# Two steps of a long convolution, interleaved in batches of four units instead of two

## The chip, the cores and the metric

The kernel runs on one core of one Trainium2 chip. The metric is the device time of one launch in microseconds (us). TensorE (PE) multiplies, VectorE (DVE), ScalarE (ACT) and GpSimd (POOL) work element by element, and SyncE (SP) issues the transfers between memory and the chip's SBUF. PE writes its results to PSUM, which has eight banks of 2 KB per partition; ACT and DVE read them from there.

## The reference

Two stages follow one another. The change touches the first one only, a long convolution by Fourier transform:

```python
h_mlp = np.maximum(pos_emb @ w1, 0.0) @ w2        # the filter
u = x * v                                         # (4, 11456, 128)
Uf = np.fft.rfft(u, n=2 * S, axis=1)
Hf = np.fft.rfft(h_mlp * window, n=2 * S, axis=0)
y = np.fft.irfft(Uf * Hf[None], n=2 * S, axis=1)[:, :S, :]
attn_out = x * y
```

The second stage is a soft mixture of eight experts over the 45,824 rows of `attn_out`. All data are float32.

## The kernel before

The transform has length 111 x 197 and is done as matrix products with tables, in four steps for each of G = 8 groups of 16 channels (64 rows of batch and channel). A group's 64 rows are worked on as NU = 16 *units* of four.

- **Step 1** (`first`, matmuls on L138, copies in `first_out` on L150) transforms a unit of `u` along one axis. The operands are at most 64 x 64, so four matmuls run side by side in the four quarters of PE's array. A unit is 16 matmuls into two PSUM banks, and ACT copies each bank to the SBUF tile T.
- **Step 2** (`p2`, L279) transforms along the other axis, four columns of T at a time; DVE multiplies with the filter's spectrum Hs (L282), and POOL writes the sums back into T (L287, L288).
- **Step 3** (`p3`, matmuls L296, copies L302) is the inverse along the second axis: 8 matmuls a unit on nearly the full array (111 x 99) into two banks, each copied by ACT to the tile E.
- **Step 4** (`p4`, L331) is the inverse along the first; ACT and DVE finish it (`p4_copy` L340, `p4_gate` L345 to L356), and the result is written out.

The trace has two PE records for every matmul of the program, so a unit of step 3 is 16 records and a unit of step 1 is 32.

For g = 1 to 7, the loop first runs **step 3 of group g-1 and step 1 of group g interleaved** (below: the 3/1 stage), because a unit of step 1 writes the part of T that two units of step 3 have read. Then steps 4 of group g-1 and 2 of group g alternate (the 4/2 stage). Group 8 has only steps 3 and 4 left. Nearly every instruction is marked to keep the order in which the program writes it, so the order of each engine is the order of the code; engines wait for one another by semaphores.

In the 3/1 stage before, units go in pairs: step 3 for units 2b and 2b+1, then step 1 for the same two, for b = 0 to 7. (For b = 0, step 1's matmuls come ahead.) Behind each unit u of step 3, DVE prepares the input of step 1's unit u+2 (`p1_sd`: L229, twice L231, twice L235); behind each unit u of step 1, SP asks for x of unit u+6 (`p1_x`, L223), or of the next group's first two units. The ring `ld` of six buffers ties x of unit u+6 to the end of step 1's unit u. From b = 4 on, SP also asks for nine pieces of the group's spectrum (L391), and at the stage's end for v of the next group's first two units (L213); then DVE prepares these two units as well, ahead of its first multiplication of step 2.

PSUM is divided for good: pool `psa` has four tiles of one bank, which step 1 and step 2 use, and pool `pso` has two tiles of two banks, which step 3 and step 4 use. A tile is given out again when its last reader has finished, so step 1's unit u waits for the copies of unit u-2, and so does step 3's.

Of the kernel before, what the change touches and what calls it, by code (L numbers as in the profile page):

```python
# [11 lines left out]
F32 = mybir.dt.float32  # L12
F32R = mybir.dt.float32r
AF = mybir.ActivationFunctionType
# [7 lines left out]
J = 99  # L22
# [3 lines left out]
R = 56  # L26
RP = 64
FO = 64
G = 8
# [32 lines left out]
def conv_part(ctx, tc, cp, moe, xf, vf, xi, xe, pos, w1, w2, win, t1x, t1h, wt, t3, t4, hs, scr):  # L62
# [64 lines left out]
        eng.tensor_tensor(out=hid[:, 0, rs], in0=hb[:, :, 0], in1=hb[:, :, 1], op=ALU.add)  # L127
        nc.vector.tensor_tensor(out=hid[:, 1, rs], in0=hb[:, :, 0], in1=hb[:, :, 1], op=ALU.subtract)

    def first(g, u, sd):  # L130

        ps = [psa.tile([128, 2, 2, J], F32, tag="psa", name=f"p1_{g}_{u}_{h}") for h in range(2)]
        for i in range(2):
            for s in range(2):
                for h in range(2):
                    js = slice(RP * h, RP * h + JH)
                    for d in range(2):
                        steady(g, nc.tensor.matmul(  # L138
                            ps[h][RP * d : RP * d + RP, i, s, :], lhsT=sd[js, i, s, d, :],
                            rhs=tab1x[js, J * (s + d) : J * (s + d + 1)],  # L140
                            start=True, stop=True, tile_position=(RP * h, RP * d)))
        return ps

    def first_out(g, u, ps):

        for h in range(2):
            dst = T[:, :, 2 * (u % 2) + h, u // 2]
            src = ps[h].rearrange("p c s k -> p s k c")
            if g or h == 0:
                steady(g, nc.scalar.activation(dst, src, AF.Copy))  # L150
            else:
                inorder(nc.vector.tensor_copy(out=dst, in_=src))
# [51 lines left out]
    def p1_v(g, u):  # L204
        k = u % HV if g == 0 else u - PRE
        if 0 <= k < HV:
            vt = Hs.rearrange("p k x -> p (k x)")[:, 8 * R * k : 8 * R * k + 8 * R]
        elif HV <= k < NU - 3:
            vt = m_half(g, k - HV)[:, : 8 * R]
        else:  # L210
            vt = ld.tile([128, 8 * R], F32, tag="lv", name=f"v_{g}_{u}", bufs=2)
        vt = vt.rearrange("p (c q r) -> p c q r", c=2, q=4)
        inorder(nc.sync.dma_start(out=vt, in_=vf[g, u]))  # L213
        vts[u] = vt

    def p1_x(g, u):
        if g == 0 and u < NU // 2:
            xt = moe.E[:, J * N1 + 8 * RP * u :][:, : 8 * RP].rearrange("p (c q r) -> p c q r", c=2, q=4)
        elif g == 0 and u >= NU - 2:
            xt = m_half(g, u).rearrange("p (c q r) -> p c q r", c=2, q=4)  # L220
        else:
            xt = ld.tile([128, 2, 4, RP], F32, tag="ld", name=f"x_{g}_{u}")
        inorder(nc.sync.dma_start(out=xt, in_=xf[g, u]))  # L223
        xts[u] = xt

    def p1_sd(g, u, eng):
        xt, vt = xts.pop(u), vts.pop(u)
        xr = xt[:, :, :, :R]
        inorder(eng.tensor_tensor(out=xr, in0=xr, in1=vt, op=ALU.mult))  # L229
        for m, op in ((0, ALU.add), (2, ALU.subtract)):  # L230
            inorder(eng.tensor_tensor(out=vt[:, :, m : m + 2], in0=xr[:, :, 0:2], in1=xr[:, :, 2:4], op=op))  # L231
        sd = xt.rearrange("p c (s d) r -> p c s d r", s=2)
        vq = vt.rearrange("p c (s q) r -> p c s q r", s=2)
        for d, op in ((0, ALU.add), (1, ALU.subtract)):
            inorder(eng.tensor_tensor(out=sd[:, :, :, d, :R], in0=vq[:, :, :, 0], in1=vq[:, :, :, 1],  # L235
                                      op=op))
        return sd
# [30 lines left out]
    for k in range(0, J, 4):  # L268
        filter_second(k)

    def p1(g, u, sd):
        first_out(g, u, first(g, u, sd))

    def p2(g, k0):
        n = min(KB, J - k0)
# [11 lines left out]
        inorder(nc.gpsimd.tensor_tensor(out=Ty[:, 0], in0=m[:, :n, 0, 0], in1=m[:, :n, 1, 1], op=ALU.subtract))  # L287
        inorder(nc.gpsimd.tensor_tensor(out=Ty[:, 1], in0=m[:, :n, 1, 0], in1=m[:, :n, 0, 1], op=ALU.add))  # L288

    def p3(g, u):  # L290
        ps = pso[0].tile([J, 2, 512], F32, tag="psb", name=f"p3_{g}_{u}")
        for k in range(2):
            pk = ps[:, k, : 8 * R].rearrange("p (i q r) -> p i q r", i=2, q=4)
            for i in range(2):
                for s in range(2):
                    inorder(nc.tensor.matmul(pk[:, i, 2 * s : 2 * s + 2, :].rearrange("p q r -> p (q r)"),  # L296
                                             lhsT=T[0:N1, s, 2 * k + i, u // 2, :, u % 2],
                                             rhs=tab3[:, 2 * R * s : 2 * R * (s + 1)],
                                             start=True, stop=True))
        for k in range(2):  # L300
            c = 4 * u + 2 * k
            inorder(nc.scalar.activation(  # L302
                E[:J, :, :, c : c + 2].rearrange("p r q c -> p q r c"),
                ps[:, k, : 8 * R].rearrange("p (i q r) -> p q r i", i=2, q=4), AF.Copy))

    AINV = pow(N1, -1, N2)

# [71 lines left out]
    for g in range(G + 1):  # L379

        if g == 0:
            for u in range(NU):
                p1(g, u, sds.pop(u))
        elif g < G:
            if not pso:
                first_ps.close()
                pso.append(ctx.enter_context(tc.tile_pool(name="pso", bufs=2, space=bass.MemoryType.PSUM)))
            for b in range(NU // 2):
                if b >= 4:
                    for k in range(11 * (2 * b - 8), min(J, 11 * (2 * b - 5 if b == 7 else 2 * b - 6)), 11):  # L390
                        inorder(nc.sync.dma_start(out=Hs[:, k : k + 11], in_=hs[g, :, k : k + 11]))  # L391
                us = (2 * b, 2 * b + 1)
                ps = {u: first(g, u, sds[u]) for u in us if b == 0}
                for u in us:
                    p3(g - 1, u)
                    if u + 2 < NU:
                        sds[u + 2] = p1_sd(g, u + 2, nc.vector)
                for u in us:
                    if b:
                        ps[u] = first(g, u, sds[u])  # L400
                    first_out(g, u, ps[u])
                    w = u + 6
                    if w < NU:
                        p1_x(g, w)
                    elif w < NU + PRE and g + 1 < G:
                        p1_x(g + 1, w - NU)
                if b == 0:
                    for w in range(PRE + HV, NU):
                        p1_v(g, w)
                if b == NU // 2 - 1 and g + 1 < G:  # L410
                    for w in range(PRE):
                        p1_v(g + 1, w)
# [641 lines left out]
```

## Time and profile before

| | us |
|---|---|
| runs: median (lowest, highest) of 3 | 947.03 (944.58, 947.36) |
| profiled execution, its own time | 946.41 |
| span of the profiled execution | 944.6 |
| one 3/1 stage and one 4/2 stage (224.00 to 262.43 and 262.43 to 307.19) | 38.43 and 44.76 |

The profile shows one execution on one core. A row of the timeline gives the start in us, the time from the first start to the last end of a run of like instructions, the engine, the line, the operation, what it writes and reads, the shape, the number of records, and in brackets the idle time ahead of it with what ended it. PEld is PE's loading of weights, which overlaps PE. The granted clock of TensorE is 0.983 of full speed on the mean over the span and 1.00 in both stages named in the table. The names are shortened there: p is any PSUM tile.

### The profile page before, as it was taken

Reading aid. Unit: us, or ns where it says so; the run is one execution under the profiler, and the core shown is the slowest. Engines: PE = TensorE matmul, PEld = TensorE weight load, DVE = VectorE, ACT = ScalarE, POOL = GpSimd, SP = SyncE. Lnnn points to the kernel's source line nnn. Section 1 sums busy time; section 2 is a strip of 40 time slices with the busy share of each in tenths; the row PEclk is TensorE's granted clock in tenths of the full one; section 3 lists DMA queues with packets and bytes.
Section 4 is the critical chain, followed back from the end, with each engine's and each line's share of the span. In section 5 each row is a group of like instructions: output and inputs, shape, how many; then the busy total and the mean of one; then the engine's idle time right before and its main releaser. Section 6 shows DMA issues by size and latency. Waiting matters only on the chain. (4 is left out here: it accounts for less than half of the span.)

```text
span 944.6 us, 32994 instructions
## 1 busy us (share of the span) xinstructions
PE 900.0 (95%) x14040; PEld 813.9 (86%) x14040; DVE 734.7 (78%) x1282; ACT 445.3 (47%) x964; POOL 381.8 (40%) x582
## 2 busy tenths in 40 slices
PE   6999999999999999999999999999999989999991
PEld 5998889999999999999999999999998987776540
DVE  7935769699789879978988998898697068876781
ACT  0655447514721751472166137216612548887561
POOL 5001760183058018405800840581085006876810
PEclk9999999999999999999999999999999999999995
DMA  8923985456745855673585568358435888775598
GB/s 267 394 71 104 325 284 173 156 169 206 240 123 160 266 156 156 194 258 111 161 274 168 152 181 257 106 173 268 142 99 164 290 300 296 259 264 158 208 417 372
DMA packets 104239, 201.18 MB, mean 213 GB/s; under 512 B 14167, under 2 KB 65577, under 8 KB 100252
## 3 DMA queue, kind: packets, MB, share of 16 engines
q1 hardware_dynamic: 103806, 198.89, 63.9%
q8 instruction: 111, 1.82, 0.8%
q14 instruction: 36, 0.29, 0.1%
q10 hardware_dynamic: 254, 0.11, 0.0%
q0 software_dynamic: 32, 0.07, 0.0%
HBM read 139.12 MB, written 59.90 MB: 211 GB/s over the span
## 5 line engine op out<-in xcount | busy, mean ns | idle before, releaser
L287 POOL TENSOR_TENSOR T<-m 111x256 f32<-111x256 f32 (+1 forms) x200 | 148.0, 740 | 424.1 <-DVE m L282 424.1
L282 DVE TENSOR_TENSOR m<-p,T 111x1024 f32<-111x1024 f32 (+1 forms) x175 | 200.1, 1207 | 22.1 <-PE p L279 21.2
L296 PE MATMUL p<-tab,T 111*99 111x112 f32 x2048 | 211.4, 262 | 2.3 <-DVE E L356 1.6
L296 PEld LDWEIGHTS p<-tab,T 111*99 111x99 f32 x2048 | 201.3, 171 | 9.7 <-issue 2.9
L279 PE MATMUL p<-T,W 128*111 128x128 f32 x1584 | 194.7, 278 | 0.0
L279 PEld LDWEIGHTS p<-T,W 128*111 128x111 f32 x1584 | 183.0, 173 | 7.3
L340 ACT ACTIVATE vc<-p 128x416 f32<-128x416 f32 x112 | 51.8, 515 | 283.9 <-DVE p L345 192.5
L331 PE MATMUL p<-tab,E 99*64 99x104 f32 x3584 | 171.9, 253 | 2.2 <-ACT E L302 1.1
L302 ACT ACTIVATE E<-p 99x448 f32<-99x448 f32 x256 | 130.5, 575 | 83.5 <-PE p L296 83.5
L331 PEld LDWEIGHTS p<-tab,E 99*64 99x64 f32 x3584 | 161.3, 136 | 9.8 <-issue 1.7
L288 POOL TENSOR_TENSOR T<-m 111x256 f32<-111x256 f32 (+1 forms) x200 | 146.6, 733 | 0.0
L150 ACT ACTIVATE T<-p 128x396 f32<-128x396 f32 x240 | 102.3, 530 | 6.7 <-PE p L138 6.6
L138 PE MATMUL p<-tab1x,x 53*64 53x99 f32 x3776 | 96.5, 248 | 3.3 <-issue 1.7
L138 PEld LDWEIGHTS p<-tab1x,x 53*64 53x64 f32 x3776 | 84.7, 133 | 10.4 <-issue 2.0
L345 DVE TENSOR_TENSOR p<-p,vc 128x832 f32<-128x832 f32 x56 | 57.4, 1025 | 14.2 <-ACT vc L340 14.2
L560 ACT ACTIVATE xreg<-pt 128x512 f32<-128x512 f32 x90 | 48.0, 602 | 5.9 <-PE pt L559 3.9
L229 DVE TENSOR_TENSOR x<-x,T 128x448 f32<-128x448 f32 x55 | 34.1, 620 | 19.7 <-DMA x<-in_xf_dram 18.8
L353 DVE TENSOR_TENSOR E<-p,E 128x824 f32<-128x824 f32 x46 | 46.8, 1017 | 1.6
L559 PE MATMUL pt<-ident,xreg 128*128 128x128 f32 x358 | 47.5, 278 | 0.0
L661 POOL TENSOR_TENSOR E<-lt,mx 128x512 f32<-128x512 f32 (+1 forms) x23 | 23.5, 1024 | 58.9 <-ACT et L642 58.9
L559 PEld LDWEIGHTS pt<-ident,xreg 128*128 128x128 f32 x358 | 40.1, 146 | 4.9 <-issue 2.4
L282 DVE TENSOR_TENSOR m<-p,E 111x1024 f32<-111x1024 f32 (+1 forms) x25 | 29.0, 1208 | 19.4 <-ACT E L186 15.3
(108 smaller groups left out, 966.6 us busy)
## 6 DMA issues: line engine op xcount, KB each, us to landing
x<-in_xf_dram SPq DMA_DIRECT2D x118, 256.0 KB, 4.1
out_dram<-xreg SPq DMA_DIRECT2D x21, 1024.0 KB, 9.6
E<-in_xi_dram SPq DMA_DIRECT2D x46, 412.0 KB, 3.6
scr<-E SPq DMA_DIRECT2D x84, 206.0 KB, 3.3
T<-in_vf_dram SPq DMA_DIRECT2D x65, 224.0 KB, 5.3
hs<-E SPq DMA_DIRECT2D x12, 1024.0 KB, 5.1
T<-hs SPq DMA_DIRECT2D x63, 176.0 KB, 3.7
mv<-in_vf_dram SPq DMA_DIRECT2D x42, 224.0 KB, 5.1
```

Of the source, the lines that this page charges most:

```text
L138: steady(g, nc.tensor.matmul(ps[h][RP * d : RP * d + RP, i, s, :], lhsT=sd[js, i, s, d, :], rhs=tab1x[js, J * (s + d) : J * (s + d + 1)], ...
L150: steady(g, nc.scalar.activation(dst, src, AF.Copy))
L279: steady(g, nc.tensor.matmul(ps[:, i].rearrange("p b c -> p (b c)"), lhsT=W[:, k0 + i, :], rhs=Tf[:, :, k0 + i, :], start=True, stop=True))
L282: inorder(nc.vector.tensor_mul(m[:, :n].rearrange("p k s e c i -> p k s (e c i)").rearrange("p k s (b c) -> p k s b c", c=CG), ps[:, :n].u ...
L287: inorder(nc.gpsimd.tensor_tensor(out=Ty[:, 0], in0=m[:, :n, 0, 0], in1=m[:, :n, 1, 1], op=ALU.subtract))
L288: inorder(nc.gpsimd.tensor_tensor(out=Ty[:, 1], in0=m[:, :n, 1, 0], in1=m[:, :n, 0, 1], op=ALU.add))
L296: inorder(nc.tensor.matmul(pk[:, i, 2 * s : 2 * s + 2, :].rearrange("p q r -> p (q r)"), lhsT=T[0:N1, s, 2 * k + i, u // 2, :, u % 2], rhs ...
L302: inorder(nc.scalar.activation(E[:J, :, :, c : c + 2].rearrange("p r q c -> p q r c"), ps[:, k, : 8 * R].rearrange("p (i q r) -> p q r i", ...
L331: inorder(nc.tensor.matmul(pv[RP * h : RP * h + RP, 2 * k + i, w, :], lhsT=E[:J, r, 2 - 2 * w + s, :], rhs=tab4[:, s, o : o + NJ], start=( ...
L340: inorder(nc.scalar.activation(vc[:, w], pv[:, :, 0, :], AF.Copy, scale=2.0 * w - 1.0))
L345: inorder(nc.vector.tensor_tensor(out=pw, in0=pw[:, 1:2].to_broadcast([128, 2, 4, NJ]), in1=vc, op=ALU.add))
L559: inorder(nc.tensor.transpose(pt[:, j, :], self.xt[i][:, k + j, :], self.ident))
```

## The change

In the 3/1 stage, units now go in batches of four: step 3 for units 4b to 4b+3, then step 1 for the same four, for b = 1 to 3. The first four units keep their order of two and two. To have eight banks for a batch, both steps now take tiles of both pools: the first two units of a batch take one two-bank tile of `pso` each, the other two take two one-bank tiles of `psa` each. Steps 2 and 4, and step 3 of the last group, take what they took. The pieces of the spectrum are asked for four at the start of b = 2 and five at the start of b = 3.

```diff
+    def banks(g, u, name, large):
+        if large:
+            t = pso[0].tile([128, 2, 512], F32, tag="psb", name=f"{name}_{g}_{u}")
+            return [t[:, h] for h in range(2)]
+        return [psa.tile([128, 512], F32, tag="psa", name=f"{name}_{g}_{u}_{h}") for h in range(2)]
+
-    def first(g, u, sd):
+    def first(g, u, sd, large=False):
-        ps = [psa.tile([128, 2, 2, J], F32, tag="psa", name=f"p1_{g}_{u}_{h}") for h in range(2)]
+        ps = [t[:, : 4 * J].rearrange("p (c s k) -> p c s k", c=2, s=2) for t in banks(g, u, "p1", large)]
...
-    def p3(g, u):
-        ps = pso[0].tile([J, 2, 512], F32, tag="psb", name=f"p3_{g}_{u}")
+    def p3(g, u, large=True):
+        ps = [t[:J, : 8 * R] for t in banks(g, u, "p3", large)]
...
-            for b in range(NU // 2):
-                if b >= 4:
-                    for k in range(11 * (2 * b - 8), min(J, 11 * (2 * b - 5 if b == 7 else 2 * b - 6)), 11):
-                        inorder(nc.sync.dma_start(out=Hs[:, k : k + 11], in_=hs[g, :, k : k + 11]))
-                us = (2 * b, 2 * b + 1)
-                ps = {u: first(g, u, sds[u]) for u in us if b == 0}
-                for u in us:
-                    p3(g - 1, u)
-                    if u + 2 < NU:
-                        sds[u + 2] = p1_sd(g, u + 2, nc.vector)
-                for u in us:
-                    if b:
-                        ps[u] = first(g, u, sds[u])
-                    first_out(g, u, ps[u])
...
+            def third(us, larges):
+                for u, large in zip(us, larges):
+                    p3(g - 1, u, large)
                     if u + 2 < NU:
                         sds[u + 2] = p1_sd(g, u + 2, nc.vector)
...
+            third(range(2, 4), (True, True))
+            for u in range(2, 4):
+                p1(g, u, sds[u])
+                behind(u)
+            for b in range(1, NU // 4):
+                if b > 1:
+                    spectrum(4 * b - 8, 5 * b - 6)
+                us = range(4 * b, 4 * b + 4)
+                third(us, (True, True, False, False))
+                for u in us:
+                    p1(g, u, sds[u], u % 4 < 2)
+                    behind(u)
```

`behind(u)` holds the loads of x that stood in the old loop, `spectrum` the loads of Hs.

How PE's own order changes is shown where the old order left units 4 and 5 (group 2). Here `p1_2_5` is step 1 of group 2, unit 5 (the last digit after it, if any, is the bank), and `p3_1_6` is step 3 of group 1, unit 6. Before:

```order
L138 MATMUL p1_2_5_0_2984<-tab1x_74,x_2_5_2405 64x99 x2
L138 MATMUL p1_2_5_1_2985<-tab1x_74,x_2_5_2405 64x99 x2
L296 MATMUL p3_1_6_3006<-tab3_75,T_78 99x112 x8
L296 MATMUL p3_1_7_3022<-tab3_75,T_78 99x112 x8
L138 MATMUL p1_2_6_0_3038<-tab1x_74,x_2_6_2837 64x99 x2
L138 MATMUL p1_2_6_1_3039<-tab1x_74,x_2_6_2837 64x99 x2
```

Now, from the batch's first unit to its first two units of step 1:

```order
L302 MATMUL p3_1_4_2930<-tab3_75,T_78 99x112 x8
L302 MATMUL p3_1_5_2946<-tab3_75,T_78 99x112 x8
L302 MATMUL p3_1_6_0_2962<-tab3_75,T_78 99x112 x4
L302 MATMUL p3_1_6_1_2963<-tab3_75,T_78 99x112 x4
L302 MATMUL p3_1_7_0_2979<-tab3_75,T_78 99x112 x4
L302 MATMUL p3_1_7_1_2980<-tab3_75,T_78 99x112 x4
L144 MATMUL p1_2_4_2996<-tab1x_74,x_2_4_2403 64x99 x16
L144 MATMUL p1_2_5_3017<-tab1x_74,x_2_5_2405 64x99 x16
```

Units 6 and 7 of step 3 moved ahead of units 4 and 5 of step 1 and write one-bank tiles. The number of matmuls is what it was.

ACT's copies of units 4 to 7 follow the same pattern. Before:

```order
L302 ACTIVATE E_79<-p3_1_4_2930 99x4x56x2 x2
L302 ACTIVATE E_79<-p3_1_5_2946 99x4x56x2 x2
L150 ACTIVATE T_78<-p1_2_4_0_2962 128x2x198
L150 ACTIVATE T_78<-p1_2_4_1_2963 128x2x198
L150 ACTIVATE T_78<-p1_2_5_0_2984 128x2x198
L150 ACTIVATE T_78<-p1_2_5_1_2985 128x2x198
L302 ACTIVATE E_79<-p3_1_6_3006 99x4x56x2 x2
L302 ACTIVATE E_79<-p3_1_7_3022 99x4x56x2 x2
L150 ACTIVATE T_78<-p1_2_6_0_3038 128x2x198
L150 ACTIVATE T_78<-p1_2_6_1_3039 128x2x198
```

Now:

```order
L308 ACTIVATE E_79<-p3_1_4_2930 99x4x56x2 x2
L308 ACTIVATE E_79<-p3_1_5_2946 99x4x56x2 x2
L308 ACTIVATE E_79<-p3_1_6_0_2962 99x4x56x2
L308 ACTIVATE E_79<-p3_1_6_1_2963 99x4x56x2
L308 ACTIVATE E_79<-p3_1_7_0_2979 99x4x56x2
L308 ACTIVATE E_79<-p3_1_7_1_2980 99x4x56x2
L156 ACTIVATE T_78<-p1_2_4_2996 128x2x198 x2
L156 ACTIVATE T_78<-p1_2_5_3017 128x2x198 x2
L156 ACTIVATE T_78<-p1_2_6_0_3038 128x2x198
L156 ACTIVATE T_78<-p1_2_6_1_3039 128x2x198
```

Eight copies to E now stand ahead of eight to T, where four and four alternated.

On SP, the second half of the stage before, where `x_2_14` is x of group 2, unit 14, and `x_3_0` that of the next group:

```order
L223 DMA x_2_13_3080<-in_xf_dram 128x512
L391 DMA T_78<-hs_57 128x352 x2
L223 DMA x_2_14_3136<-in_xf_dram 128x512
L223 DMA x_2_15_3158<-in_xf_dram 128x512
L391 DMA T_78<-hs_57 128x352 x2
L223 DMA x_3_0_3214<-in_xf_dram 128x512
L223 DMA x_3_1_3236<-in_xf_dram 128x512
L391 DMA T_78<-hs_57 128x352 x5
L213 DMA v_3_0_3377<-in_vf_dram 128x448
```

Now:

```order
L229 DMA x_2_13_3080<-in_xf_dram 128x512
L409 DMA T_78<-hs_57 128x352 x4
L229 DMA x_2_14_3171<-in_xf_dram 128x512
L229 DMA x_2_15_3192<-in_xf_dram 128x512
L229 DMA x_3_0_3214<-in_xf_dram 128x512
L229 DMA x_3_1_3236<-in_xf_dram 128x512
L409 DMA T_78<-hs_57 128x352 x5
L219 DMA v_3_0_3377<-in_vf_dram 128x448
```

Two pieces of the spectrum moved ahead of x of units 14 and 15; the five pieces behind x of the next group stand where they stood.

More of the change, by code (lines that the diff above doesn't have):

```diff
@@ L269, in conv_part, with p1 @@
         filter_second(k)
-    def p1(g, u, sd):
-        first_out(g, u, first(g, u, sd))
+    def p1(g, u, sd, large=False):
+        first_out(g, u, first(g, u, sd, large))
     def p2(g, k0):
@@ L288, in p2 @@
         inorder(nc.gpsimd.tensor_tensor(out=Ty[:, 1], in0=m[:, :n, 1, 0], in1=m[:, :n, 0, 1], op=ALU.add))
-    def p3(g, u):
-        ps = pso[0].tile([J, 2, 512], F32, tag="psb", name=f"p3_{g}_{u}")
+    def p3(g, u, large=True):
+        ps = [t[:J, : 8 * R] for t in banks(g, u, "p3", large)]
         for k in range(2):
-            pk = ps[:, k, : 8 * R].rearrange("p (i q r) -> p i q r", i=2, q=4)
+            pk = ps[k].rearrange("p (i q r) -> p i q r", i=2, q=4)
             for i in range(2):
@@ L303, in p3 @@
                 E[:J, :, :, c : c + 2].rearrange("p r q c -> p q r c"),
-                ps[:, k, : 8 * R].rearrange("p (i q r) -> p q r i", i=2, q=4), AF.Copy))
+                ps[k].rearrange("p (i q r) -> p q r i", i=2, q=4), AF.Copy))
     AINV = pow(N1, -1, N2)
@@ L396, in conv_part @@
                     if u + 2 < NU:
                         sds[u + 2] = p1_sd(g, u + 2, nc.vector)
-                for u in us:
-                    if b:
-                        ps[u] = first(g, u, sds[u])
-                    first_out(g, u, ps[u])
[L402 to L409, printed above, removed]
@@ L410, in conv_part, with behind, spectrum @@
-                if b == NU // 2 - 1 and g + 1 < G:
-                    for w in range(PRE):
-                        p1_v(g + 1, w)
+            def behind(u):
+                w = u + 6
+                if w < NU:
+                    p1_x(g, w)
+                elif w < NU + PRE and g + 1 < G:
+                    p1_x(g + 1, w - NU)
+            def spectrum(i0, i1):
+                for k in range(11 * i0, 11 * i1, 11):
+                    inorder(nc.sync.dma_start(out=Hs[:, k : k + 11], in_=hs[g, :, k : k + 11]))
@@ new lines, in conv_part @@
+            ps = [first(g, u, sds[u]) for u in range(2)]
+            third(range(2), (True, True))
+            for u in range(2):
+                first_out(g, u, ps[u])
+                behind(u)
+            for w in range(PRE + HV, NU):
+                p1_v(g, w)
+            third(range(2, 4), (True, True))
[7 more added lines that the diff above has]
+                third(us, (True, True, False, False))
+                for u in us:
+                    p1(g, u, sds[u], u % 4 < 2)
+                    behind(u)
@@ L413, in conv_part @@
+            if g + 1 < G:
+                for w in range(PRE):
+                    p1_v(g + 1, w)
         else:
```

## The prediction

> **What bounds the kernel now.** I read the engines' shares on the page first, then the busy time by stage, then PE's timeline through one 3/1 stage, then the engines that could hold PE up there.
>
> ```profile
> PE 900.0 (95%) x14040; PEld 813.9 (86%) x14040; DVE 734.7 (78%) x1282; ACT 445.3 (47%) x964; POOL 381.8 (40%) x582
> ```
>
> ```profile
> 224.00:262.43 38.43, 38.31 (x770) 36.38 (x768) 31.81 (x82) 28.32 (x64) 0.32 (x1) 1.00 0.77 249
> 262.43:307.19 44.76, 44.76 (x650) 42.99 (x646) 41.78 (x44) 6.70 (x15) 34.18 (x50) 1.00 0.47 137
> ```
>
> The second fence gives, per stretch, its length and then the busy time of PE, PEld, DVE, ACT and POOL. PE is busy all through both stages (38.31 of 38.43, 44.76 of 44.76), so whatever shortens PE's own work there shortens the kernel, until another engine takes over. DVE is the nearest: 31.81 and 41.78.
>
> A busy PE may still lose time between its instructions, which is where this change acts:
>
> ```profile
> 224.00 1.61 PE L138 MATMUL p<-tab1x,x 53*64 53x99 f32 x64
> 225.53 6.72 PE L296 MATMUL p<-tab,T 111*99 111x112 f32 x64
> 232.18 1.61 PE L138 MATMUL p<-tab1x,x 53*64 53x99 f32 x64
> 233.72 3.32 PE L296 MATMUL p<-tab,T 111*99 111x112 f32 x32
> 236.97 1.61 PE L138 MATMUL p<-tab1x,x 53*64 53x99 f32 x64
> 238.51 3.31 PE L296 MATMUL p<-tab,T 111*99 111x112 f32 x32
> ...
> 260.89 1.61 PE L138 MATMUL p<-tab1x,x 53*64 53x99 f32 x64
> 262.43 3.08 PE L331 MATMUL p<-tab,E 99*64 99x104 f32 x64
> ```
>
> From one step-1 run to the next a pair takes (260.89 - 232.18) / 6 = 4.785 us: 3.25 from the start of step 3 to that of step 1, and 1.54 back. How much of it is matmul? These rows are pieces from inside a run, and the long run of step 3 in the last group, which no step 1 interrupts:
>
> ```profile
> 234.29 2.46 PE L296 MATMUL p<-tab,T 111*99 111x112 f32 x24
> 237.11 1.30 PE L138 MATMUL p<-tab1x,x 53*64 53x99 f32 x52
> 726.94 23.22 PE L296 MATMUL p<-tab,T 111*99 111x112 f32 x240 [0.91 <-DVE E L356]
> L296 PE MATMUL p<-tab,T x2048: 259/259/507, 141.5 to 749.9; 111*99 111x112 f32 x187
> L138 PE MATMUL p<-tab1x,x x3776: 242/244/370, 76.8 to 678.6; 53*64 53x99 f32 x199
> ```
>
> A record of step 3 takes 0.259 us from start to end, so 24 of them start (2.46 - 0.26) / 23 = 0.0957 us apart; over 240 it is 0.0961. Step 1's records start in fours: 52 are 13 fours, and the step from four to four is between (1.30 - 0.24) x 4 / 51 = 0.083 and (1.30 - 0.24) / 12 = 0.088; I take 0.086. A pair is then 32 x 0.0957 + 16 x 0.086 = 3.06 + 1.38 = 4.44 us of matmul. **The other 0.345 us (0.31 to 0.39 by the two bounds) is what changing from step 3 to step 1 and back costs.** It is no wait for data: it is the same in every pair, and the copies that the next run needs are long done, as follows.
>
> **What the change removes.** The matmuls stay the same 14,040 records. Before, each stage goes back and forth seven times after the first run (b = 1 to 7); now four times (units 2-3, then three batches). Three round trips fewer, in seven stages: 21 x 0.345 = **7.2 us** (6.5 to 8.2). A batch takes 64 x 0.0957 + 32 x 0.086 + 0.345 = 9.22 us in place of 9.57.
>
> **What it moves on ACT and PSUM.** Now a batch's step-1 units want the banks of its step-3 units, and the next batch's step 3 those of step 1.
>
> ```profile
> 233.42 1.74 ACT L150 ACTIVATE T<-p 128x396 f32<-128x396 f32 x4
> 235.55 1.02 ACT L302 ACTIVATE E<-p 99x448 f32<-99x448 f32 x2 [0.38 <-PE p L296]
> 237.08 1.04 ACT L302 ACTIVATE E<-p 99x448 f32<-99x448 f32 x2 [0.51 <-PE p L296]
> 237.99 1.67 ACT L150 ACTIVATE T<-p 128x396 f32<-128x396 f32 x4
> ```
>
> A unit's two copies to E take 1.04 us and start 0.11 after PE's run of step 3 (237.08 against 236.97); its two copies to T take half of 1.67, 0.84. Counted from a batch's start, step 1 begins at 3.25 + 32 x 0.0957 = 6.31. The fourth unit's copies to E end at 6.42 + 1.04 = 7.46, and its banks are wanted again by step 1's fourth unit at 6.31 + 0.73 + 2 x 0.69 = 8.42 (8 fours, 0.69 us a unit, and 0.04 more for the first): 0.96 to spare. Copies to T end at 8.30, 9.14, 9.98 and 10.82; the next batch's four step-3 units want those tiles at 9.22, 10.76, 12.29 and 13.82: 0.92 to spare at the least. Behind the last batch step 2 starts after step 4's 3.01 us, at 12.23, with T complete at 10.82. ACT needs 4 x (1.04 + 0.84) = 7.5 of 9.22. So I cost this at nothing; the cover is about 0.9 us a batch. One missing bank would cost like the one wait that the stage has today, where step 3's second unit waits for step 4's last reader:
>
> ```profile
> 227.13 0.15 DVE L356 TENSOR_TENSOR E<-p,E 128x4 f32<-128x4 f32 x1
> 227.40 4.67 PEld L296 LDWEIGHTS p<-tab,T 111*99 111x99 f32 x48 [0.27 <-issue]
> ```
>
> That is 0.27 us on PEld, and it stays: 64 x 0.0957 and 0.19 for the change of step (3.25 - 3.06) leave 6.65 - 6.31 = 0.34 us in that run.
>
> **What it moves on SP and DVE.** x of unit u+6 is asked for when step 1's unit u is done, and units 4, 5, 8 and 9 are now done some 3 us later. DVE prepares in unit order, 2.0 us a unit:
>
> ```profile
> 242.21 0.63 DVE L229 TENSOR_TENSOR x<-x,T 128x448 f32<-128x448 f32 x1 [2.96 <-DMA x<-in_xf_dram]
> 246.27 0.62 DVE L229 TENSOR_TENSOR x<-x,mv 128x448 f32<-128x448 f32 x1
> 250.32 0.62 DVE L229 TENSOR_TENSOR x<-x,mv 128x448 f32<-128x448 f32 x1
> 254.38 0.62 DVE L229 TENSOR_TENSOR x<-x,mv 128x448 f32<-128x448 f32 x1
> 260.39 0.63 DVE L229 TENSOR_TENSOR x<-x,v 128x448 f32<-128x448 f32 x1 [1.94 <-PE p L296]
> 263.77 0.69 DVE L235 TENSOR_TENSOR x<-v 128x224 f32<-128x224 f32 x2
> 266.65 2.36 DVE L282 TENSOR_TENSOR m<-p,T 111x1024 f32<-111x1024 f32 x2 [2.18 <-PE p L279]
> ```
>
> ```profile
> 235.83 7.94 SPq L223 DMA_DIRECT2D x<-in_xf_dram  x6
> 247.54 1.02 SPq L223 DMA_DIRECT2D x<-in_xf_dram  x2
> 256.54 2.27 SPq L213 DMA_DIRECT2D v<-in_vf_dram  x2
> x<-in_xf_dram SPq DMA_DIRECT2D x118, 256.0 KB, 4.1
> T<-hs SPq DMA_DIRECT2D x63, 176.0 KB, 3.7
> ```
>
> The rows at 242.21, 246.27, 250.32 and 254.38 begin units 8, 10, 12 and 14. In this stage the batches would start at 233.72, 242.94 and 252.16, and step 4 at 261.40. x of unit 10 is asked for at 233.72 + 6.31 + 0.73 = 240.8 and lands, by the median of 4.1, at 244.9, ahead of its 246.27. x of unit 14 is asked for at 242.94 + 7.04 = 250.0 (247.54 before) and lands at 254.1, ahead of 254.38. So DVE's row of preparations hardly moves. Its closest user is step 1's unit 11, wanted at 242.94 + 8.42 = 251.36 and ready at 250.32. In the latest stage DVE began unit 8 later, and PE already waited for unit 9 there (1.85 for 1.61):
>
> ```profile
> 400.12 3.32 PE L296 MATMUL p<-tab,T 111*99 111x112 f32 x32
> 409.67 0.62 DVE L229 TENSOR_TENSOR x<-x,T 128x448 f32<-128x448 f32 x1 [4.03 <-DMA x<-in_xf_dram]
> 412.94 1.85 PE L138 MATMUL p<-tab1x,x 53*64 53x99 f32 x64
> ```
>
> That 0.24 falls away, since unit 9 moves back to 400.12 + 9.22 + 7.04 = 416.4; unit 11 takes its place with nothing to spare (ready at 409.67 + 8.1 = 417.8, wanted at 400.12 + 9.22 + 8.42 = 417.8). I set the two against each other. At the end, step 2's first product is now wanted 1.03 earlier, at 265.62, and DVE's last preparation ends at 263.77 + 0.69 = 264.46. The v ahead of it stands on SP behind the same loads as now, and step 1's units 12 to 15 release nothing there, so I take it as asked for no later than now (256.54). DVE has some slack behind that, where it waits at the 4/2 stage's end:
>
> ```profile
> 386.88 2.09 DVE L282 TENSOR_TENSOR m<-p,T 111x1024 f32<-111x1024 f32 x2 [0.39 <-PE p L279]
> 391.47 1.03 DVE L345 TENSOR_TENSOR p<-p,vc 128x832 f32<-128x832 f32 x1 [0.45 <-ACT vc L340]
> ```
>
> **The sum.** 946.41 (the profiled execution) - 7.2 = 939.2; the median of the runs lies 0.6 higher, which gives 939.8. I predict 939.5 us.
>
> **Rivals.**
>
> *A bank comes late.* If ACT's copies ran 0.9 us behind the sums above, each batch would begin one run with a wait of 0.27 to 0.35 us, the price of today's: 21 x 0.27 to 0.35 = 5.7 to 7.4, and the time would be 945 to 946.6. For it: the spare time is only a tenth of a batch. Against it: ACT waits for PE at every E copy in the rows above, and would keep 1.7 us a batch. [...]
>
> *The 0.345 belongs to the units, not to the change of step* (a cost at each new tile, say). Then nothing is saved: 946.4. The run of 240 records speaks against it: 15 units in a row, at 0.0961.
>
> *DVE is late in part.* If it loses half a microsecond a stage at unit 11 or at step 2's start, 3.5 of the 7.2 go: 943.
>
> *Slower: the loads of the second half bunch up.* Four pieces of spectrum now stand ahead of x of units 14 and 15, and v behind four x and five pieces. Let x of unit 14 and v take 6.4 us, as x of unit 8 does today (235.83 to 242.21). Unit 14 is prepared from 256.4, unit 15 to 260.4; the second v needs unit 15's buffer, so it lands at 266.8 and DVE is free at 268.8, 2.15 later than step 2's product starts today. Less the slack of 0.39 + 0.45 that is 1.3 us in each of seven stages, because DVE's 41.78 busy of 44.76 leaves no room to catch up: 946.4 + 9.2 = 955.6. It decides from 267.5 on, 3.0 us after today's 264.46. Against it: the pieces that are moved forward are asked for from 243 on and, by their median of 3.7 us, there ahead of 250.
>
> **Numbers.** Forecast 0.75; DVE late in part 0.07 (faster still); bank late 0.07 and no saving 0.05 (both same); bunched loads 0.06 (slower). With 0.3%, about 2.8 us, as what a measurement of this kernel can tell from no change: faster 0.82, same 0.12, slower 0.06. The range of the forecast alone is 946.41 - 8.2 to 947.03 - 6.5, so 938.2 to 940.5; three runs before lay up to 2.4 below their median, and partial losses reach 943, so I give 936.8 to 943.5.
>
> **What would show it.** In the profile after: three runs of 64 records of step 3 per stage, each about 6.3 us from its start to step 1's, and runs of 128 of step 1, 2.9 us; 82.2 us from group to group (83.2 now); no idle time of PE ahead of these rows. I am wrong if the runs of 128 stretch (a bank or DVE late), or if DVE's first product of a 4/2 stage stands behind a preparation without idle time.

## The result, and the profile after

| | before | after |
|---|---|---|
| median of 6 runs each (lowest, highest), us | 945.58 (943.66, 947.36) | 938.98 (937.37, 942.66) |
| profiled execution, its own time, us | 946.41 | 938.47 |
| span of the profiled execution, us | 944.6 | 936.7 |
| mean granted clock of TensorE | 0.983 | 0.988 |

The ratio is 0.9928 with a 95% interval of 0.9899 to 0.9957: 0.7% faster, 4 to 10 us of 945.6. The forecast was 939.5.

PE's timeline through one 3/1 stage of the changed kernel (columns: start, length, engine, line, operation, operands, shape, number of records):

```profile
469.06 1.61 PE L144 MATMUL p<-tab1x,x 53*64 53x99 f32 x64
470.60 6.72 PE L302 MATMUL p<-tab,T 111*99 111x112 f32 x64
477.25 1.61 PE L144 MATMUL p<-tab1x,x 53*64 53x99 f32 x64
478.79 6.38 PE L302 MATMUL p<-tab,T 111*99 111x112 f32 x64
485.10 2.98 PE L144 MATMUL p<-tab1x,x 53*64 53x99 f32 x128
488.01 6.38 PE L302 MATMUL p<-tab,T 111*99 111x112 f32 x64
494.32 2.98 PE L144 MATMUL p<-tab1x,x 53*64 53x99 f32 x128
497.24 6.38 PE L302 MATMUL p<-tab,T 111*99 111x112 f32 x64
503.55 2.99 PE L144 MATMUL p<-tab1x,x 53*64 53x99 f32 x128
```

A batch takes 488.01 - 478.79 = 9.22 us: 6.31 from the start of step 3 to that of step 1, and 2.91 back. No row has idle time ahead of it. This is the busy time by stage of another group, where nothing disturbs it either (length of the stretch, then busy time of PE, PEld, DVE, ACT and POOL with their records, the granted clock, the DMA share and GB/s):

```profile
551.23:588.64 37.41, 37.30 (x770) 36.08 (x768) 31.82 (x82) 28.96 (x64) 0.33 (x1) 1.00 0.78 246
588.64:633.40 44.76, 44.76 (x650) 42.98 (x646) 41.81 (x44) 6.87 (x16) 34.20 (x50) 1.00 0.47 140
```

The 3/1 stage is 1.02 shorter than before (38.43) with the same records on PE, DVE and ACT, and the 4/2 stage is what it was (44.76). In such a group the whole gain lies where the order was changed, and none of it is given back in the next stage.

Where did the 7.9 us between the two profiles come from? I take the first record of step 3 in each stage as a mark. From mark to mark:

```
first mark           before 141.49                                        after 138.36
group to group, before  84.04  83.20  83.20  83.43  83.20  83.27  82.44   sum 582.78
group to group, after   83.29  83.08  82.17  83.69  82.17  82.17  81.41   sum 577.98
from the last mark to the span's end           before 220.3, after 220.3
```

An undisturbed group fell from 83.20 to 82.17, and the last from 82.44 to 81.41: 1.03 each, seven times, 7.2 us. The sums differ by only 4.8, because after has more disturbances (1.12, 0.91 and 1.52 in its first, second and fourth group, together 3.55) than before (0.84, 0.23 and 0.07, together 1.14). The other 3.13 us stand ahead of the first mark, in work that the change does not touch. In the other profiles in which the work up to there is the same, that mark lies anywhere from 139.0 to 141.9; the changed kernel itself has it at 138.36 here and at 140.55 in the repetition below. So that part is chance, and another execution could have made the profiled pair look 3 us worse. The medians are the safer measure: 6.6 us here, 7.3 in the repetition below.

Rows of the profile show where the three disturbances lie, all but some 0.3 us of the first. The first two rows are from the second group, the next two from the fourth, and the last from the first group's 4/2 stage (idle time and what ended it in brackets; "issue" means that the profile shows nothing that PE waited for):

```profile
245.39 2.30 PE L144 MATMUL p<-tab1x,x 53*64 53x99 f32 x96
248.09 1.17 PE L144 MATMUL p<-tab1x,x 53*64 53x99 f32 x32 [0.41 <-ACT T L156]
...
401.42 2.97 PE L144 MATMUL p<-tab1x,x 53*64 53x99 f32 x127
405.67 0.24 PE L144 MATMUL p<-tab1x,x 53*64 53x99 f32 x1 [1.28 <-issue]
...
178.04 0.40 PE L337 MATMUL p<-tab,E 99*64 99x104 f32 x3 [0.63 <-issue]
```

The wait at 248.09 is unit 11 of step 1. The profile names ACT, but DVE tells what was late:

```profile
240.10 0.62 DVE L235 TENSOR_TENSOR x<-x,T 128x448 f32<-128x448 f32 x1 [2.72 <-DMA x<-in_xf_dram]
...
247.60 0.69 DVE L241 TENSOR_TENSOR x<-mv 128x224 f32<-128x224 f32 x2
```

DVE waited for x of unit 8 until 240.10 and then prepared units 8, 9, 10 and 11 without a pause. Unit 11's last two operations start at 247.60, the first of them is done about 247.98, and PE goes on at 248.09. The waits marked "issue" are the subject of the last section.

### The profile page after: what moved, and what is told of

Same layout as the page of the kernel before. It is cut to its first block, busy times and chain, and to the rows that moved or that the text cites. A ratio compares the mean times of both kernels' runs of the same rounds, so it can differ in the third digit from the quotient of the medians.

```text
span 936.7 us, 33000 instructions
## 1 busy us (share of the span) xinstructions
PE 890.1 (95%) x14040; PEld 810.6 (87%) x14040; DVE 734.5 (78%) x1282; ACT 451.0 (48%) x964; POOL 382.0 (41%) x582
## 3 DMA queue, kind: packets, MB, share of 16 engines
q8 instruction: 111, 1.82, 0.8%
## 5 line engine op out<-in xcount | busy, mean ns | idle before, releaser
L302 PE MATMUL p<-tab,T 111*99 111x112 f32 x2048 | 205.3, 260 | 2.6 <-DVE E L362 1.6
L302 PEld LDWEIGHTS p<-tab,T 111*99 111x99 f32 x2048 | 198.8, 170 | 9.1 <-issue 2.7
L337 PE MATMUL p<-tab,E 99*64 99x104 f32 x3584 | 172.2, 253 | 2.8 <-ACT E L308 1.1
L337 PEld LDWEIGHTS p<-tab,E 99*64 99x64 f32 x3584 | 161.5, 136 | 10.5 <-issue 2.4
L308 ACT ACTIVATE E<-p 99x448 f32<-99x448 f32 x256 | 132.6, 575 | 65.4 <-PE p L302 64.1
L156 ACT ACTIVATE T<-p 128x396 f32<-128x396 f32 x240 | 100.6, 537 | 12.4 <-PE p L144 12.2
L144 PE MATMUL p<-tab1x,x 53*64 53x99 f32 x3776 | 91.5, 247 | 3.3 <-DVE m L288 1.5
L144 PEld LDWEIGHTS p<-tab1x,x 53*64 53x64 f32 x3776 | 83.6, 132 | 6.8 <-DVE m L288 1.7
```

The source lines that it names most:

```text
L144: steady(g, nc.tensor.matmul(ps[h][RP * d : RP * d + RP, i, s, :], lhsT=sd[js, i, s, d, :], rhs=tab1x[js, J * (s + d) : J * (s + d + 1)], ...
L308: inorder(nc.scalar.activation(E[:J, :, :, c : c + 2].rearrange("p r q c -> p q r c"), ps[k].rearrange("p (i q r) -> p q r i", i=2, q=4), ...
L337: inorder(nc.tensor.matmul(pv[RP * h : RP * h + RP, 2 * k + i, w, :], lhsT=E[:J, r, 2 - 2 * w + s, :], rhs=tab4[:, s, o : o + NJ], start=( ...
```

## The experiments

Lines L144, L302 and L337 are steps 1, 3 and 4 of the changed kernel, L156 and L308 ACT's copies to T and to E. The shared banks have the same lines in all its variants.

### The changed kernel again

No edit.

> The changed kernel once more, beside the kernel before. Theory (21 changes of step and back saved at 0.345 us, and two or three random waits given back): 938 to 940 us, 6 to 8 below the kernel before; groups of 82.2 us from one step 3 to the next, but for those in which step 1's unit 11 waits for DVE. If the 1.4 us wait of PE at the very end of one run of step 1 (group 4) belongs to the new order, it stands there again; if it is chance, it is somewhere else or nowhere.

940.14 us (938.99 to 944.21, 10 runs) against 947.43 for the kernel before on the same chip (25 runs): ratio 0.9929 (0.9904 to 0.9953). Undisturbed groups are 82.17 again. Unit 11's wait is small this time (the run of 128 in the third group takes 3.12 for 2.98). The wait in the fourth group came back, at the same two records as in the profile above:

```profile
406.39 2.97 PE L144 MATMUL p<-tab1x,x 53*64 53x99 f32 x127
409.89 0.24 PE L144 MATMUL p<-tab1x,x 53*64 53x99 f32 x1 [0.54 <-issue]
```

### More changes of step instead of fewer

The kernel before, with step 1 of a unit straight behind step 3 of that unit: the round trips between the steps go from 7 to 14 a stage, and tiles, units and matmuls stay.

```diff
                 for u in us:
                     p3(g - 1, u)
                     if u + 2 < NU:
                         sds[u + 2] = p1_sd(g, u + 2, nc.vector)
+                    if b:
+                        ps[u] = first(g, u, sds[u])
                 for u in us:
-                    if b:
-                        ps[u] = first(g, u, sds[u])
                     first_out(g, u, ps[u])
```

> The kernel before, with step 1's matmuls of a unit straight behind step 3's of that unit, the copies as before: each pair of units (b = 1 to 7) goes to step 1 and back twice instead of once, with the same tiles, the same matmuls and the same loads. Theory (a change of step and back costs 0.345 us): 49 more of them, 16.9 us slower than the kernel before, about 962.5. Rival (the 0.345 belongs to units or new tiles): no change, 945.6. A pair would take 5.13 us instead of 4.785 by the theory.

966.6 us (964.41 to 968.33), ratio 1.0203 (1.0165 to 1.0242). PE's timeline, with L296, L138 and L331 for steps 3, 1 and 4:

```profile
318.05 1.30 PE L138 MATMUL p<-tab1x,x 53*64 53x99 f32 x32
...
320.99 0.92 PE L138 MATMUL p<-tab1x,x 53*64 53x99 f32 x32
321.85 1.78 PE L296 MATMUL p<-tab,T 111*99 111x112 f32 x16
323.56 0.92 PE L138 MATMUL p<-tab1x,x 53*64 53x99 f32 x32
...
352.94 2.28 PE L331 MATMUL p<-tab,E 99*64 99x104 f32 x46 [0.26 <-ACT E L302]
```

From 320.99 to 323.56 is 2.57 a unit; over the twelve units from 320.99 to 351.77 it is 5.13 a pair, where the kernel before has 4.785: 0.345 more for one more round trip. A stage is 3.12 longer: 7 x 0.345, 0.38 in the first run of step 1, which is stretched (1.30 where the others take 0.92: a bank that comes late, behind ACT's copies to T from 317.50 on) and 0.33 ahead of step 4, which now waits for the last copy to E. I had counted the round trips alone, so the time is 4 us above my 962.5. If the 0.345 belonged to the units or tiles, the pair would have stayed at 4.785. That rival falls.

The rows give the price of changing from step 3 to step 1 and back, 0.345 us. What PE does in that time, no run here shows.

### The order without the shared banks

The changed kernel with the banks of before: step 3 in the two two-bank tiles, step 1 in the four one-bank tiles, in batches of four all the same.

```diff
-                third(us, (True, True, False, False))
+                third(us, (True, True, True, True))
                 for u in us:
-                    p1(g, u, sds[u], u % 4 < 2)
+                    p1(g, u, sds[u])
```

> The changed kernel's batches of four, but step 3 in two-bank tiles alone and step 1 in one-bank tiles alone, as before the change. Theory: step 1's third and fourth unit now wait for the copies of the first two, which stand behind eight copies to E: the fourth unit starts at about 9.2 us of a batch instead of 8.42, so a batch takes some 9.95 us, 0.7 more than with shared banks and 0.4 more than two pairs: 21 x 0.4 = 8 slower than the kernel before, about 953. Rival (order is all, banks do not matter): as the changed kernel, 939.

956.24 us (953.25 to 957.6), ratio 1.0093 (1.0066 to 1.012): slower than the kernel before. PE, and ACT at the same place:

```profile
405.65 6.38 PE L302 MATMUL p<-tab,T 111*99 111x112 f32 x64
411.96 3.63 PE L144 MATMUL p<-tab1x,x 53*64 53x99 f32 x128
415.53 6.38 PE L302 MATMUL p<-tab,T 111*99 111x112 f32 x64
```

```profile
412.07 1.01 ACT L308 ACTIVATE E<-p 99x448 f32<-99x448 f32 x2 [0.51 <-PE p L302]
412.96 3.43 ACT L156 ACTIVATE T<-p 128x396 f32<-128x396 f32 x8
```

The run of step 1 takes 3.63 instead of 2.98, a batch 9.88. ACT copies the last unit of step 3 first and begins the copies to T at 412.96, a full microsecond into PE's run; step 1's third and fourth units want the banks of its first two, which ACT frees only from 413.8 on. Three batches at 9.88 against 9.57 for two pairs of before are 0.93 a stage, and the undisturbed groups show it: 84.1 against 83.2. So the saved round trip (0.345) is outweighed by the wait for a bank (0.66). The order alone loses; it needs the eight banks. The rival "a bank comes late" described a real mechanism, and what kept it out is the bank plan.

### Unit 11 without its wait

In the changed kernel, the loads of v that stand on SP ahead of x of units 8 and 9 move behind them.

```diff
             for u in range(2):
                 first_out(g, u, ps[u])
                 behind(u)
-            for w in range(PRE + HV, NU):
-                p1_v(g, w)
             third(range(2, 4), (True, True))
             for u in range(2, 4):
                 p1(g, u, sds[u])
                 behind(u)
+            for w in range(PRE + HV, NU):
+                p1_v(g, w)
```

> The changed kernel with x of units 8 and 9 asked for ahead of the seven v loads of units 9 to 15 instead of behind them. Theory (unit 11's wait for DVE in two of seven stages comes from x of unit 8 landing late behind 1.6 MB of v): DVE starts unit 8 some 3 us sooner, no wait at unit 11 in any stage, 0.5 to 1.5 us below the changed kernel. Rival (the v loads are then late for unit 9 and on): waits at units 9 to 11, 1 to 5 us slower.

940.9 us (938.8 to 943.26, 12 runs), ratio 0.9936 (0.9915 to 0.9956). The second group, where unit 11 had waited, and what came instead at its end:

```profile
250.33 2.98 PE L144 MATMUL p<-tab1x,x 53*64 53x99 f32 x128
...
265.52 1.47 PE L337 MATMUL p<-tab,E 99*64 99x104 f32 x26 [1.04 <-issue]
```

The run of 128 is 2.98 again, and no run of units 8 to 11 is stretched in any group. DVE begins unit 8 of this group 13.6 us after the group's mark, where it was 18.4 in the profile after, so unit 11's wait did come from the late x. The 0.5 to 1.5 us that I had expected below the changed kernel did not show: the profile has two "issue" waits, here and at 182.99, and the time is that of the changed kernel. Unit 11 was worth 0.9 us in one profile of the changed kernel and less in the other, which is less than runs differ by.

### The stream shifted

The "issue" waits came at the same records twice. If they belong to a place in PE's stream of instructions, issuing more instructions early must move them to other records. 32 matmuls of the filter, before the first group, are issued twice; the second time writes the same values.

```diff
-            for h in range(2):
+            for h in (range(2) if f >= 16 else (0, 1, 0, 1)):
```

> The changed kernel with 32 matmuls of the filter's first step issued twice (same result), so that every later PE instruction stands 128 places further back in its stream. In the changed kernel and its repeat, PE stood still for 0.8 to 1.5 us at the same instructions (three records before the end of a step-4 run in group 1, one before the end of a step-1 run in group 4), and each of these has the place 193 or 194 modulo 256 in PE's stream, behind a 16 KB instruction transfer. Theory (PE waits there for its own instructions, in blocks of 256): no such wait at those two instructions; any wait of over 0.6 us without a data releaser in the interleaved stages stands again at 193 to 195 modulo 256, so at other matmuls. Rival (something in the new order holds just those instructions up): the waits stay at the same two matmuls. Time within 3 us of 940.

947.37 us (945.53 to 949.43), ratio 1.001 (0.9997 to 1.0023). As a time the expectation (within 3 of 940) missed: the first mark moved to 147.03, some 7 us behind the 138 to 142 of the others, so the doubled matmuls lengthened the first phase by more than I had costed. As a test of the place it is clear. The first two rows are the records at which the two kernels above waited, the others are where this one waits:

```profile
411.86 2.98 PE L144 MATMUL p<-tab1x,x 53*64 53x99 f32 x128
414.77 6.38 PE L302 MATMUL p<-tab,T 111*99 111x112 f32 x64
...
579.12 1.78 PE L302 MATMUL p<-tab,T 111*99 111x112 f32 x16
581.57 2.62 PE L302 MATMUL p<-tab,T 111*99 111x112 f32 x25 [0.67 <-PE p L302]
659.28 2.86 PE L144 MATMUL p<-tab1x,x 53*64 53x99 f32 x121
662.78 0.40 PE L144 MATMUL p<-tab1x,x 53*64 53x99 f32 x7 [0.64 <-issue]
```

No wait at the old records, and two at others. (At 581.57 the bracket names PE itself: no load and no other engine.) Four groups in a row are exactly 82.17, which is the change's gain without disturbance.

### The wait of step 3's second unit taken away

A try at a better kernel: only one unit of step 1 runs ahead of a stage, step 3's second unit takes one-bank tiles, and the wait of 0.34 us for step 4's last reader goes. (x stands ahead of v, as above.)

```diff
-            ps = [first(g, u, sds[u]) for u in range(2)]
-            third(range(2), (True, True))
-            for u in range(2):
-                first_out(g, u, ps[u])
-                behind(u)
+            ps = first(g, 0, sds[0])
+            third(range(2), (True, False))
+            first_out(g, 0, ps)
+            behind(0)
+            third(range(2, 4), (True, True))
+            for u in range(1, 4):
+                p1(g, u, sds[u], u == 1)
+                behind(u)
             for w in range(PRE + HV, NU):
                 p1_v(g, w)
-            third(range(2, 4), (True, True))
-            for u in range(2, 4):
-                p1(g, u, sds[u])
-                behind(u)
```

> The changed kernel with only unit 0 of step 1 ahead of step 3 at the start of a 3/1 stage instead of units 0 and 1; step 3's unit 1 takes two one-bank tiles, step 1's unit 1 a two-bank tile; x of units 8 and 9 are asked for ahead of the seven v loads. As many changes of step as the changed kernel. Theory (step 3's second unit waits 0.34 us in each stage for step 4's last reader to free its two-bank tile): that wait is gone in all seven stages, groups of 81.83 us instead of 82.17, 2.4 us faster than the changed kernel, about 937.5. Rival (DVE, which frees that tile, is itself the bound, and another wait takes the place): groups stay at 82.17.

939.93 us (939.46 to 944.09), ratio 0.9943 (0.9926 to 0.9959): no different from the changed kernel. First the start of a stage, then the end of one:

```profile
555.35 6.38 PE L302 MATMUL p<-tab,T 111*99 111x112 f32 x64
561.66 2.30 PE L144 MATMUL p<-tab1x,x 53*64 53x99 f32 x96
...
261.40 2.00 PE L337 MATMUL p<-tab,E 99*64 99x104 f32 x39
264.81 1.38 PE L337 MATMUL p<-tab,E 99*64 99x104 f32 x25 [1.41 <-issue]
```

Step 3's first run of 64 is 6.38 where it was 6.72, and undisturbed groups take 81.83, 0.34 less, as expected. The time, which I had put at about 937.5, did not follow: in the profiled execution three "issue" waits (1.63 at 182.25, 1.66 at 264.81, 1.24 at 409.55, as spaces between two records) cost 4.5 us, more than the 2.4 that seven stages can save. Whether the other executions have as many is not known.

### The spectrum's loads in one bunch

The changed kernel with all nine pieces of the spectrum asked for at the third batch, ahead of all that follows on SP. Nine pieces then stand ahead of x of units 14 and 15 where the changed kernel has four: more of what the slower rival feared for x. (The loads of v that follow have the same loads ahead of them as in the changed kernel.)

```diff
-                if b > 1:
-                    spectrum(4 * b - 8, 5 * b - 6)
+                if b == 2:
+                    spectrum(0, 9)
```

> The changed kernel with all nine pieces of the spectrum asked for at the start of b = 2, ahead of x of units 14 and 15, so 1.6 MB stand ahead of them. Theory (x of unit 14 is asked for 7 us after those pieces and DVE has time): groups stay at 82.17 us, 938 to 941. Rival (the second half's loads decide: DVE gets to step 2's first product late): 1 to 1.5 us more a group, 946 to 950.

942.11 us (939.6 to 944.05, 5 runs), ratio 0.9953 (0.9934 to 0.9971), 1.1 above the 938 to 941 that I had expected. The run of units 8 to 11 is stretched in two groups, of which this is one (2.98 where it is undisturbed), and an "issue" wait stands at 407.72:

```profile
496.37 3.60 PE L144 MATMUL p<-tab1x,x 53*64 53x99 f32 x128
```

The groups but for the first and the last are 82.17 to 83.0. The rival's 946 to 950 was not reached, so bunched loads at this place cost about 1 to 2 us, if anything, and the 955.6 falls (the changed kernel's own 938.98 had ruled it out already).

### The loads of v early

The kernel of one unit ahead, with seven loads of v straight behind x of unit 6 and so ahead of x of units 7 to 9.

```diff
             first_out(g, 0, ps)
             behind(0)
+            for w in range(PRE + HV, NU):
+                p1_v(g, w)
             third(range(2, 4), (True, True))
             for u in range(1, 4):
                 p1(g, u, sds[u], u == 1)
                 behind(u)
-            for w in range(PRE + HV, NU):
-                p1_v(g, w)
```

> The kernel with one unit of step 1 ahead (e6), with the seven v loads back ahead of x of units 7 to 9. Theory (the 0.34 us wait of step 3's second unit is gone, and what took its place in e6 are three waits of PE for its own instructions, which differ from run to run): groups of 81.83 us where no such wait stands, 936 to 940 us, 0 to 3 below the changed kernel. Rival (x of unit 8 is late again behind the v loads): a wait of 0.5 us or so at unit 11 in two stages, else the same.

957.18 us (954.88 to 962.26), ratio 1.0129 (1.01 to 1.0158), some 17 above the same kernel with x first. I had expected 936 to 940 and was wrong. SP's queue, then DVE, then PE:

```profile
230.93 2.75 SPq L219 DMA_DIRECT2D mv<-in_vf_dram  x6
...
234.25 9.98 SPq L229 DMA_DIRECT2D x<-in_xf_dram  x7
```

```profile
240.68 0.63 DVE L235 TENSOR_TENSOR x<-x,T 128x448 f32<-128x448 f32 x1 [4.61 <-PE p L144]
```

```profile
242.57 1.28 PE L144 MATMUL p<-tab1x,x 53*64 53x99 f32 x32 [1.75 <-DVE x L241]
243.78 7.88 PE L302 MATMUL p<-tab,T 111*99 111x112 f32 x64
```

x of unit 7 is asked for at 234.25, behind the seven v (one more row of them is left out), and 6.4 us later, at 240.65, it lands; the median of the loads of x around it is 3.4. DVE starts on it at 240.68, so it was the load that it waited for and not the PE that the bracket names, and step 1's unit 7 waits for DVE. The same unit waits in six of the seven stages (1.10 to 2.31 from one record to the next, together 11.7 us). That is not all that such a wait costs. The run of step 3 behind it takes 7.88 us instead of 6.38: from 243.5 to 246.9 the granted clock is 0.50, and the run's first record takes 0.51 where step 3's take 0.26. The same happens behind the waits at 328.59 and 498.79, about 1.6 us each, and not behind the other three. So a load that comes late for a unit with no slack cost 1 to 2 us in each of six stages, and in three of them the clock took as much again: that is what the slower rival would have looked like.

### The loads of v early, and the stream shifted

The same, with step 1's first unit of group 1 issued three times (the same values each time), which moves the place of the "issue" waits.

```diff
-        for i in range(2):
+        for i in (range(2) if g != 1 or u else (0, 1, 0, 1, 0, 1)):
```

> e8 with step 1's first unit of group 1 issued three times (same result), where PE waits some 1.8 us anyway: 128 more PE instructions ahead of all the rest. Theory (PE takes its instructions in blocks of 256 and waits at places 193 to 195 modulo 256 when a dense run uses a block up before the next has come): the waits of e8 leave their matmuls and stand at others, again at 193 to 195 of the stream; undisturbed groups 81.83; 936 to 941 us. Rival: the waits stay at the matmuls where e6 and e8 have them.

952.96 us (946.17 to 958.14, 12 runs), ratio 1.0073 (1.0047 to 1.0099), where I had expected 936 to 941. Unit 7 waits here too (0.8 to 2.9), and the times differ so much from run to run that the comparison with the kernel above says little. As a test of the place it has no partner: the profile of the kernel above has no "issue" wait of over 0.6 us that could have moved. There is one here (519.03, step 4). No version that I ran is shown to beat the changed kernel.

## Why the prediction was right, point by point

**The 0.345 us of a round trip.** Right in size and cause. Three fewer a stage save 1.03 (predicted 3 x 0.345 = 1.035), and seven more cost 7 x 0.345. The batch took 9.22, as predicted, the group 82.17 for 82.2.

**ACT and PSUM at no cost.** Right, and the spare time is somewhat larger than worked out. ACT through a batch that starts at 560.96:

```profile
564.32 2.11 ACT L308 ACTIVATE E<-p 99x448 f32<-99x448 f32 x4 [0.51 <-PE p L302]
566.62 0.56 ACT L308 ACTIVATE E<-p 99x448 f32<-99x448 f32 x1 [0.19 <-PE p L302]
567.38 0.57 ACT L308 ACTIVATE E<-p 99x448 f32<-99x448 f32 x1 [0.21 <-PE p L302]
568.26 3.25 ACT L156 ACTIVATE T<-p 128x396 f32<-128x396 f32 x8 [0.31 <-PE p L144]
```

The last copy to E ends at 567.95, 6.99 after the batch's start, where I had 7.46: in a one-bank tile the first copy starts when the first bank is written, not the unit. The copies to T end at 571.51, 10.55 for my 10.82. "The cover is about 0.9 us" held, and the order without the shared banks showed what stands behind it: 0.66 a batch. With all eight banks shared a batch is 9.22. With four banks for each step it is 9.88, because the copies come in an order that frees a bank late.

**The 0.34 us wait that stays.** Right: the first run of 64 is 6.72 where the others are 6.38, and removing its cause gave 81.83.

**DVE and the loads.** Right that DVE's row hardly moves and that unit 11 is the closest ("nothing to spare"). To "set the two against each other" was too kind: in the profile after, x of unit 8 came later and unit 11 waited 0.9 us in one group, where before lost 0.24 at unit 9. The end of the stage was right; step 2's first product still stands behind idle time of DVE, 2.15 us (2.18 before):

```profile
592.86 2.36 DVE L288 TENSOR_TENSOR m<-p,T 111x1024 f32<-111x1024 f32 x2 [2.15 <-PE p L285]
```

**"No idle time of PE ahead of these rows".** True of five groups of seven, wrong in two: unit 11, and a wait of 1.28 us for no data at all, which no step of the prediction had.

**The sum.** 7.2 us was the undisturbed gain and 6.6 the gain of the medians, whose interval is wider than the difference. Of the profiled execution's 7.9, only 4.8 lie between the marks. That the forecast came within 0.5 us of the measured time is in part luck: it started from a profile of 946.41 and a median of 947.03 over three runs, and over six runs that median is 945.58.

**The rivals.** No saving (946.4): excluded by the split steps and by the undisturbed groups. A bank late (945 to 946.6): the mechanism is real, the banks of the change prevent it. DVE late in part (943): 0.9 us in one group instead of 0.5 in each. Bunched loads (955.6): not even with all nine pieces at once; a late x for a unit without slack did cost that much (957.18), at another place.

## What to carry to other kernels

When PE is busy all through a stage, compare the time from run to run with the spacing of the records inside the runs: what was left over here, 0.345 us of 4.785 in a pair, was the price of changing from one kind of matmul to another, and three changes there and back fewer took back 1.03 us a stage. Longer runs need the PSUM banks to match: count for each bank when its last copy ends and when it is wanted again, since here the same order gained 0.7% with shared banks and lost 0.9% without. A saving of some microseconds can hide in, or be faked by, what differs from execution to execution, so read it from undisturbed groups and not from the difference of two spans.

## What was unexpected: PE waits for its own instructions

The page's line of the queue that carries instructions (packets, MB, share of 16 engines) in the profile after:

```profile
q8 instruction: 111, 1.82, 0.8%
```

1.82 MB in 111 packets are 16.4 KB each. PE has 14,040 matmul, 14,040 weight-load and 349 other records (346 of them of semaphores), together 28,429; if all 111 packets are PE's, that is 256 a packet, and 64 bytes each. I counted the place in this stream, modulo 256, of each space of over 0.6 us in the 3/1 and 4/2 stages that no data explain (given as the space between two matmul starts; in the last column the start of the 16 KB packet that came before):

```
kernel           at      space  step  place  packet at
after            178.04  0.88   4     193    175.77
after            405.67  1.53   1     193    403.38
changed again    183.29  0.90   4     193    181.08
changed again    409.89  0.78   1     193    407.28
order only       184.39  0.83   2     194    181.96
order only       352.06  1.41   4     194    348.84
order only       500.06  0.92   1     194    497.66
x first          182.99  0.64   4     193    180.71
x first          265.52  1.29   4     194    263.25
stream shifted   581.57  0.93   3     195    578.96
stream shifted   662.78  0.89   1     194    660.33
one ahead        182.25  1.63   4     194    179.86
one ahead        264.81  1.66   4     194    262.54
one ahead        409.55  1.24   3     194    407.16
spectrum bunched 168.92  0.75   3     193    166.61
spectrum bunched 181.35  0.65   4     193    179.10
spectrum bunched 407.72  0.85   1     193    405.39
v early, shifted 519.03  1.66   4     194    516.68
```

All 18 stand at place 193 to 195 of 256, whatever step is running there, and nearly all end 2.2 to 2.6 us after a packet starts (the longest 3.2). So I take these for waits for the next block of instructions: a packet holds 256 of them by the count above, and the places agree modulo 256.

That a shifted stream moved the waits to other records at the same place is shown. Why some blocks come late and most don't, the traces show in part: the transfer itself begins late. In the eleven profiles 849 of these packets start between 138 and 716 us. Those ahead of the 18 waits start 0.6 to 1.8 us before PE has come to place 193, the other 831 start 1.7 us or more before (median 6.6). None starts more than 293 instructions ahead of that place. From this earliest point to the start of the packet the 18 took 2.7 to 4.6 us, where the median of all is 1.7.

In that time the DMA engines were busy. These rows are of the kernel with one unit ahead, the first from the earliest point to the start of the packet at 262.54, the second with PE's wait, which ends at 264.81 (the DMA share is the number ahead of the GB/s):

```profile
258.90:262.54 3.64, 3.64 (x146) 3.52 (x140) 2.35 (x6) 3.33 (x9) 0.00 (x0) 1.00 0.83 274
262.00:264.80 2.80, 1.40 (x31) 1.20 (x27) 2.12 (x6) 0.71 (x2) 0.00 (x0) 1.00 0.13 45
```

The share is 0.83 ahead of the packet's start and 0.13 in the second row, where PE waits. In the time ahead of the start it is 0.73 to 1.05 for all 18, while the 219 packets that started less than 1 us after their earliest point have a median share of 0.00 there. So a packet seems to start late when the DMA engines are full of other transfers. No run changed that traffic alone, so this is suggested and not shown.

The one profile of the kernel before has no such wait in its 3/1 and 4/2 stages, nor have that of the split steps and that with v early, and the kernel before has one of 1.83 us at the same place in its dense first group. A run of 128 records of step 1 with its weight loads is 256 instructions in 2.9 us, while before no more than 128 came in 1.54 us between two runs of step 3. That longer runs of short matmuls make a late block more likely is an argument from these numbers, not shown: step 4 and step 3 have such waits too, and the kernel with v early has the long runs and no such wait in its one profile.

The second thing was the clock. In these rows (140 to 145 us of the kernel before, the changed kernel, and the changed kernel again) the number ahead of the DMA share is the granted clock:

```profile
140.00:145.00 5.00, 4.79 (x52) 4.56 (x53) 4.86 (x12) 0.51 (x2) 1.60 (x2) 0.66 0.92 269
```

```profile
140.00:145.00 5.00, 5.00 (x54) 5.00 (x53) 4.83 (x13) 3.80 (x9) 0.00 (x0) 1.00 0.87 303
```

```profile
140.00:145.00 5.00, 4.75 (x42) 4.29 (x35) 4.83 (x12) 0.78 (x2) 1.19 (x2) 0.58 1.03 303
```

It dipped to 0.66 before, not at all in the profile after, and to 0.58 in the same kernel's repetition. The first groups of these two executions of the changed kernel differ by 3.1 us (83.29 and 86.36), most of it by this dip. The prediction named the mean clock of 0.983 and did not look where it was low, though the row of 0.66 could be read from the profile before. Why it dips there in most of the profiles and not in all stays open.
